# Loading w_in in rows of 128 in a fused attention, gated MLP and soft mixture kernel

## The chip, the cores and the metric

The kernel runs on one core of a Trainium2 chip. The metric is the device time of one execution in microseconds, the median of the runs.

## What is computed

Three layers follow each other in float32: a causal attention with a decay per head, in blocks with a running state; an MLP with a gate; and a soft mixture of eight small experts.

```python
# q, k, v: [2, 8, 768, 64]; lam: [8]
intra = einsum('bhic,bhjc->bhij', qb, kb) * Dmask     # lam ** (i - j), i >= j
inter = einsum('bhid,bhde->bhie', qb * lam_pow, kv_state)
out[:, :, sl] = einsum('bhij,bhjd->bhid', intra, vb) + inter
kv_state = lam_block * kv_state + einsum('bhsd,bhse->bhde', kb * rev_pow, vb)
# x: [1536, 512], a column is 64 * head + d
h = x @ w_in                                          # [512, 2048]
x = (h * clip(h + 3, 0, 6) / 6) @ w_out               # [2048, 512]
# soft mixture: 8 experts of 4 slots, w1 [8, 512, 1024], w2 [8, 1024, 512]
logits = x @ phi; d = softmax(logits, 0); c = softmax(logits, 1)
out = c @ experts(d.T @ x)
```

`w_in` and `w_out` arrive as float64, 8 MB each; the kernel makes float32 of them on the chip. The rest is float32.

## The kernel before, in words

**Tiles.** The 1536 tokens are 12 tiles t of 128 (six of each batch). Attention works with a block C = 128. `w_in` is cut into NF = 4 groups n of 512 columns and KT = 4 slices kt of 128 rows of the contraction; the 16 pieces are loaded as raw pairs of int32 words (`load_w_in`, L433), 4 KB a row, and turned to float32 by ScalarE and VectorE in `convert` (L577: L583, L590, L597, L604), then split in two float32r parts `whi` and `wlo` (L622). One unit h(t, n) is 12 matmuls of 128x512 (`h_unit`, L1008), in two halves of 6.

**Attention of a tile** (`attention`, L774). q and k arrive as [128 tokens, 8 heads, 64] (`load_qkv`, L409). TensorE transposes pairs of heads (L793), so a pair lies in the two halves of the partitions; ScalarE copies them out (`tr`, L810). `ps` are the scores of both halves (L862), `pm` the scores times the decay mask (VectorE, L870), `pv` the products that update the state (L883, weights k times `rev`, moving v), `px` the output, from the state (L900) and from `pm` (L907). x then has the heads in rows: slice kt holds two heads, one in each half of the partitions. `lamq` and `rev` hold powers of lam for the heads; `selp` places them (L350).

Before, the transposed pair is heads 2a and 2a+1, while slice kt of x holds heads kt and kt+4. So the rows of w_in that belong to a slice are two runs of 64, and `load_w_in` issues two transfers of 64 rows for each piece (L435 to L441). The 64x64 products with the state take their operands from the half h2 of the pair.

**Order.** Every step is an `Op` with an engine, a number in the order in which it was made, its dependencies and buffers. `ORDER` (L73) is a list of these 943 numbers written out by hand; `Plan.run` (L187) walks it, gives out ring buffers (46 of 4 KB a partition) with a table of assumed durations, and issues. So each engine's program has the order of the list. DMA issues marked `free` go to SP, or to ACT when their number is in `BY_ACT` (L123). All other loads go to SP's queue. A transfer's issue waits on SP for its buffer.

**The start of SP's list before:** w_in (0,1) as two transfers, k of tile 0, w_in (0,0) and (1,0), `pw_d` (a store of the powers of lam), q0, k1, w_in (0,3) and (0,2), q1, the two halves of the mask `dec` (read back from `pw_d`), v0, q2, k2, v1, k3, q3, w_in (1,1), v2, k4, q4, w_in (1,3), (1,2), (3,0), v3, w_in (2,0), (3,2), q7, q5, k5, and so on.

**The end.** After the last h units the experts' weights (64 loads of 512 KB on 128 rows, L1322 and L1332) are multiplied, and the result is stored.

Of the kernel before, what the change touches and what calls it, by code (L numbers as in the profile page):

```python
# [121 lines left out]
)  # L122
BY_ACT = (421, 709, 885, 918, 939,)  # L123
# [134 lines left out]
def attn_moe_softmoe_kernel(  # L258
# [60 lines left out]
    T = {}  # L319
# [15 lines left out]
    while m < C:  # L335
# [18 lines left out]
        base=0, pattern=[[-2, NPAIR], [-1, 2], [0, 64]], channel_multiplier=1,  # L354
# [57 lines left out]
    def load_qkv(x, t):  # L412
        b, c = divmod(t, NC)
        name, i = {"q": ("qk", 0), "k": ("qk", 1), "v": ("vd", 0)}[x]

        def fn():
            if (name, t) not in T:
                T[name, t] = rtile([128, 2, H, D], f"{name}{t}")
            QUEUE[plan.eng].dma_start(  # L419
                out=T[name, t][:, i],  # L420
                in_={"q": q, "k": k, "v": v}[x][b, :, C * c : C * c + C].rearrange(
                    "h p d -> p h d"
                ),
            )

        take = [] if (name, t) in bufs else [ring_buf((name, t))]
        ops["ld" + x, t] = load(
            fn, KB512 / 2, take=take, rel=[] if take else [bufs[name, t]], eff=0.58, rows=64,
            **queue(f"{x}{t}"),
            reserve=load_reserve,  # L430
        )

    def load_w_in(n, kt):  # L433
        def fn():
            T["wraw", n, kt] = rtile([128, 512, 2], f"wraw{n}_{kt}", I32)  # L435
            for i in range(2):
                r = D * (KT * i + kt)
                QUEUE[plan.eng].dma_start(  # L438
                    out=T["wraw", n, kt][D * i : D * i + D].rearrange("p f w -> p (f w)"),
                    in_=w_in.bitcast(I32)[r : r + D, 1024 * n : 1024 * n + 1024],  # L440
                )  # L441

        ops["ldw", n, kt] = load(
            fn, KB512, take=[ring_buf(("wraw", n, kt))], reserve=load_reserve, eff=1.1, n=2,
            **queue(f"w{n}_{kt}"),
        )
# [87 lines left out]
    def make_rev():  # L534
        DVE.tensor_copy(rev, T.pop("rev_p"))  # L535
# [238 lines left out]
    def attention(t, prio):  # L774
# [91 lines left out]
        def f_pm(g):  # L866
            def fn():
                if ("pm", t) not in T:
                    T["pm", t] = rtile([128, H, C], f"pm{t}")
                DVE.tensor_tensor(  # L870
                    out=T["pm", t].rearrange("p (a g) c -> p g a c", g=2)[:, g],
                    in0=T["ps", t][g],
                    in1=T["dec"].rearrange("p (a g) c -> p g a c", g=2)[:, g], op=ALU.mult,
# [4 lines left out]
        def f_pv():  # L878
            vd = T["vd", t]
            pv = T["pv", t] = ptile(v_tag, [128, NPAIR, D], f"pv{t}")  # L880
            for h in range(H):
                p, h2 = divmod(h, 2)
                PE.matmul(  # L883
                    pv[64 * h2 : 64 * h2 + 64, p], lhsT=vd[:, 1, h], rhs=vd[:, 0, h],
                    start=True, stop=True,
                )

        def bank(kt):
            return T["px", t, kt % 2][:, kt // 2] if c > 0 else T["px", t, 0][:, kt]

        def f_px():
# [4 lines left out]
            for kt in range(KT if c > 0 else 0):  # L896
                for i in range(2):
                    p, h2 = divmod(KT * i + kt, 2)
                    r = slice(64 * h2, 64 * h2 + 64)
# [824 lines left out]
```

## Time and profile before

| | us |
|---|---|
| median of 3 runs | 309.9 (309.62 to 311.62) |
| the profiled execution | 310.75 |
| its span, first to last instruction | 308.9 |
| TensorE (PE) busy | 277.1 |
| VectorE (DVE) busy | 198.8 |
| ScalarE (ACT) busy | 122.8 |
| mean granted clock of TensorE | 0.955 |

The profile is of one execution. PE are matmuls, PEld weight loads, SPq the instructions of SP's queue (DMA issues). L-numbers are lines of the kernel. Start times count from the span's start. In the table by stretch, the columns are the stretch, its length, then for PE, PEld, DVE, ACT and POOL the busy time (and count), the granted clock of TensorE as a share of full speed, the mean busy share of the 16 DMA engines, and GB/s. "[7.82 <-X]" at the end of a timeline row is the idle time of the engine before it, and what ended it. A float32 matmul shows as two instructions.

### The profile page before, as it was taken

How to read it: one execution, taken by the hardware profiler on the slowest of the kernel's cores; microseconds unless marked ns; L12 is line 12 of the kernel's file. 1: busy time of each engine (PE TensorE's matmuls, PEld its weight loads, DVE VectorE, ACT ScalarE, POOL GpSimd, SP SyncE). 2: the span in 40 equal slices, each digit the busy share in tenths (PEclk: the TensorE clock that was granted, in tenths of full speed). 3: DMA queues.
4: the chain of work that ended last, by engine and by line, in shares of the span. 5: the costliest groups of instructions: out<-in, count | busy, mean ns of one | idle time of the engine just before them, and what ended most of it. 6: DMA issues, size and time to landing. Idle time of an engine off the chain costs nothing.

```text
span 308.9 us, 7313 instructions
## 1 busy us (share of the span) xinstructions
PE 277.1 (90%) x2956; PEld 210.1 (68%) x2956; DVE 198.8 (64%) x330; ACT 122.8 (40%) x235; POOL 36.3 (12%) x51
## 2 busy tenths in 40 slices
PE   6269994999879899999999999999999998979990
PEld 5268883878657788788667768668776756556670
DVE  3368894799946999998987796675633216213151
ACT  3454555988347657312131232224124241111240
POOL 4034210423202602000110010100000000000000
PEclk9578998899959999999999999999999999999997
DMA  7999999999996765667896768999799999999987
GB/s 145 221 234 210 208 213 179 241 293 317 219 215 181 249 181 153 168 155 191 194 262 162 205 152 197 227 306 358 243 334 417 395 408 342 389 407 407 313 262 235
DMA packets 79217, 78.67 MB, mean 255 GB/s; under 512 B 41800, under 2 KB 67920, under 8 KB 79184
## 3 DMA queue, kind: packets, MB, share of 16 engines
q1 hardware_dynamic: 76704, 76.37, 88.1%
q10 hardware_dynamic: 2480, 1.84, 2.1%
q8 instruction: 23, 0.38, 0.5%
q14 instruction: 10, 0.08, 0.1%
HBM read 60.36 MB, written 3.15 MB: 206 GB/s over the span
## 4 chain that ended last, share of the span: by engine, by line
PE 63%; DMA 17%; SPq 10%; DVE 4%; issue 1%; ACT 1%; POOLq 0%; DVEq 0%; ACTq 0%
PE h L1019 35%; SPq L419 5%; SPq L438 4%; DMA wo_raw<-in_moe_w_out_dram 4%; PE po L1574 4%; DMA e<-in_moe_w_dram 4%; PE lg L1125 3%; DMA qk<-in_q_dram 3%; PE p L1540 3%; PE pd L1240 3%; PE ps L862 3%; DMA wraw<-in_moe_w_in_dram 2%; PE pt L793 2%; PE px L907 2%; DMA qk<-in_k_dram 2%; DMA gq<-gb 2%
## 5 line engine op out<-in xcount | busy, mean ns | idle before, releaser
L1019 PE MATMUL h<-whi,x 128*128 128x512 f32 x384 | 124.1, 405 | 0.6 <-DVE g L1039 0.6
L1019 PEld LDWEIGHTS h<-whi,x 128*128 128x128 f32 x384 | 70.8, 191 | 17.6 <-issue 2.0
L1019 PE MATMUL h<-wlo,x 128*128 128x512 f32 x192 | 75.9, 395 | 0.0
L1033 ACT ACTIVATE g<-h,half_b 128x512 f32<-128x512 f32 x48 | 33.0, 688 | 53.1 <-PE h L1019 37.4
L1039 DVE SCALAR_TENSOR_TENSOR g<-g,h 128x512 f32<-128x512 f32 x48 | 32.6, 678 | 29.3 <-ACT g L1033 25.9
L1102 DVE STREAM_TRANSPOSE gb<-g 128x1024 f32<-128x1024 f32 x20 | 40.9, 2053 | 5.3 <-POOL vd L849 2.5
L1019 PEld LDWEIGHTS h<-wlo,x 128*128 128x128 f32 x192 | 36.6, 191 | 8.3
L793 PE MATMUL pt<-ident,qk 128*128 128x128 f32 x96 | 15.8, 308 | 13.8 <-DMA qk<-in_q_dram 13.8
L793 PEld LDWEIGHTS pt<-ident,qk 128*128 128x128 f32 x96 | 12.1, 155 | 17.4 <-DMA qk<-in_q_dram 8.0
L931 POOL TENSOR_TENSOR states<-states,lamq 64x256 f32<-64x256 f32 x16 | 10.7, 669 | 88.9 <-DVE states L944 80.7
L810 ACT COPY tr<-pt 128x512 f32<-128x512 f32 x24 | 13.6, 582 | 17.9 <-PE pt L793 9.5
L870 DVE TENSOR_TENSOR pm<-ps,dec 128x512 f32<-128x512 f32 x24 | 15.7, 681 | 7.2 <-ACT tmp_o L590 4.0
L862 PE MATMUL ps<-tr 64*128 64x128 f32 x192 | 15.9, 306 | 3.2 <-ACT tr L810 3.0
L862 PEld LDWEIGHTS ps<-tr 64*128 64x128 f32 x192 | 13.3, 207 | 7.1 <-ACT tr L810 3.5
L583 ACT ACTIVATE tmp_i<-wraw 128x512 f32<-128x512 f32 x16 | 10.5, 670 | 18.9 <-DMA wraw<-in_moe_w_in_dram 14.5
L1559 DVE STREAM_TRANSPOSE ht<-hsi 128x256 f32<-128x256 f32 x8 | 5.1, 651 | 19.6 <-ACT hsi L1551 19.6
L1540 PE MATMUL p<-e,hsi 128*32 128x256 f32 x256 | 15.2, 381 | 2.1 <-DMA e<-in_moe_w_dram 1.6
L710 DVE STREAM_TRANSPOSE wb<-wo_f 128x1024 f32<-128x1024 f32 x8 | 16.1, 2022 | 0.1
L849 POOL TENSOR_TENSOR vd<-qk,rev 128x512 f32<-128x512 f32 x10 | 11.0, 1112 | 42.8 <-DVE rev L535 12.8
L1574 PE MATMUL po<-e,ht 128*32 128x128 f32 (+1 forms) x384 | 15.4, 309 | 0.3 <-DMA e<-in_moe_w_dram 0.3
L633 POOL TENSOR_TENSOR wlo<-tmp_i,whi 128x512 fp32r<-128x512 f32 x8 | 11.2, 1419 | 25.4 <-ACT whi L630 25.3
L1574 PEld LDWEIGHTS po<-e,ht 128*32 128x32 f32 x384 | 11.1, 110 | 4.4 <-DMA e<-in_moe_w_dram 0.5
(115 smaller groups left out, 341.9 us busy)
## 6 DMA issues: line engine op xcount, KB each, us to landing
e<-in_moe_w_dram SPq DMA_DIRECT2D x64, 512.0 KB, 7.1
gq<-gb SPq DMA_DIRECT2D x76, 128.0 KB, 2.8
wraw<-in_moe_w_in_dram SPq DMA_DIRECT2D x32, 256.0 KB, 6.6
wo_raw<-in_moe_w_out_dram SPq DMA_DIRECT2D x16, 512.0 KB, 6.0
wq<-wb SPq DMA_DIRECT2D x28, 128.0 KB, 2.7
qk<-in_k_dram SPq DMA_DIRECT2D x12, 256.0 KB, 5.8
qk<-in_q_dram SPq DMA_DIRECT2D x12, 256.0 KB, 7.0
vd<-in_v_dram SPq DMA_DIRECT2D x12, 256.0 KB, 7.3
```

Of the source, the lines that this page charges most:

```text
L419: QUEUE[plan.eng].dma_start(out=T[name, t][:, i], in_={"q": q, "k": k, "v": v}[x][b, :, C * c : C * c + C].rearrange("h p d -> p h d"),)
L710: DVE.transpose(out=x.rearrange("p q d c f -> p c d q f"), in_=y.rearrange("p c (d t q) -> p c d q t", d=KT, q=4),)
L793: PE.transpose(p[:, a], x[:, i, 2 * a : 2 * a + 2].rearrange("p a d -> p (a d)"), ident,)
L810: ACT.copy(T["tr", t][:, i], T["pt", t, i])
L862: PE.matmul(ps[g][:, p], lhsT=z[r, p], rhs=y[r, p], start=True, stop=True)
L870: DVE.tensor_tensor(out=T["pm", t].rearrange("p (a g) c -> p g a c", g=2)[:, g], in0=T["ps", t][g], in1=T["dec"].rearrange("p (a g) c -> p ...
L1019: PE.matmul(ph, lhsT=xt[:, a, kt], rhs=T[w, n, part][:, kt % 2], start=i == 0, stop=i == 3 * KT - 1,)
L1033: ACT.activation(T["g", tp, n][:, i], T["h", t, n], AF.Relu, bias=half_b, scale=1.0 / 6.0)
L1039: DVE.scalar_tensor_tensor(out=to, in0=to, scalar=1.0, in1=T.pop(("h", t, n)), op0=ALU.min, op1=ALU.mult,)
L1102: DVE.transpose(out=x.rearrange("p q c i t -> p i c q t"), in_=T["g", tp, n].rearrange("p i (c t q) -> p i c q t", c=4, q=4),)
L1540: PE.matmul(p1[32 * j : 32 * j + 32], lhsT=T["sit"][:, b4], rhs=T["e1", e, b4][:, 256 * j : 256 * j + 256], start=b4 == 0, stop=b4 == 3,)
L1574: PE.matmul(T["po", hf][32 * qd : 32 * qd + 32], lhsT=T["ht", e // 4][:, e % 4, b8], rhs=T["e2", e, b8 // 2][:, b8 % 2, lo:hi] if e < WHOL ...
```

## The change

- `load_w_in`: one transfer of 128 rows for a piece, instead of two of 64.
- `load_qkv`: q and k by two transfers each, of four heads. Heads h and h+4 stand side by side, so the pair that is transposed is (a, a+4). v stays one transfer.
- `make_rev`, `selp`, `f_pm`: the same sizes with the new order of heads.
- `f_pv`: heads 0 to 3 go to the lower half of the partitions of `pv`, heads 4 to 7 to the upper; the loop still counts h up.
- `f_px`: kt in the order 0, 2, 1, 3 for the products with the state; the two PSUM banks now hold slices (0, 1) and (2, 3) instead of (0, 2) and (1, 3).
- `ORDER` and `BY_ACT` are new. The start of SP's list: k0, w_in (0,1), q0, `pw_d`, k1, q1, w_in (0,0), (0,2), the first half of `dec`, v0, q2, k2, w_in (0,3), v1, k3, q3, w_in (1,2), v2, (1,0), k4, q4, (1,1), v3, (1,3), (3,0), two pieces of w_out, (3,2), q5, v4, k5. The second half of `dec` (number 8) is issued by ACT, after the two conversions of w_in (0,1) and ahead of the copy of q0's transposes. On TensorE the operations ahead of the first h are the same set. The transposes of tile 5 stood behind seven halves of h units, and stand behind ten.

```diff
 ORDER = (
-    10, 0, 252, 253, 2, 9, 246, 248, 247, 73, 18, 6, 4, 76, 270, 254, 77, 255, 3, 271,
+    73, 0, 76, 74, 77, 2, 75, 10, 252, 4, 6, 3, 5, 253, 254, 255, 78, 9, 11, 7,
...
 )
-BY_ACT = (421, 709, 885, 918, 939,)
+BY_ACT = (8, 409, 626, 703, 885, 918,)
...
-        base=0, pattern=[[-2, NPAIR], [-1, 2], [0, 64]], channel_multiplier=1,
+        base=0, pattern=[[-1, NPAIR], [-4, 2], [0, 64]], channel_multiplier=1,
...
-            QUEUE[plan.eng].dma_start(
-                out=T[name, t][:, i],
-                in_={"q": q, "k": k, "v": v}[x][b, :, C * c : C * c + C].rearrange(
-                    "h p d -> p h d"
-                ),
-            )
+            src = {"q": q, "k": k, "v": v}[x][b, :, C * c : C * c + C].rearrange("h p d -> p h d")
+            if x == "v":
+                QUEUE[plan.eng].dma_start(out=T[name, t][:, i], in_=src)
+                return
+            to = T[name, t][:, i].rearrange("p (a g) d -> p g a d", g=2)
+            for g in range(2):
+                QUEUE[plan.eng].dma_start(
+                    out=to[:, g], in_=src[:, NPAIR * g : NPAIR * g + NPAIR]
+                )
...
-            for i in range(2):
-                r = D * (KT * i + kt)
-                QUEUE[plan.eng].dma_start(
-                    out=T["wraw", n, kt][D * i : D * i + D].rearrange("p f w -> p (f w)"),
-                    in_=w_in.bitcast(I32)[r : r + D, 1024 * n : 1024 * n + 1024],
-                )
+            QUEUE[plan.eng].dma_start(
+                out=T["wraw", n, kt].rearrange("p f w -> p (f w)"),
+                in_=w_in.bitcast(I32)[
+                    128 * kt : 128 * kt + 128, 1024 * n : 1024 * n + 1024
+                ],
+            )
...
-                    out=T["pm", t].rearrange("p (a g) c -> p g a c", g=2)[:, g],
+                    out=T["pm", t].rearrange("p (g a) c -> p g a c", g=2)[:, g],
...
-                p, h2 = divmod(h, 2)
+                g, p = divmod(h, NPAIR)
                 PE.matmul(
-                    pv[64 * h2 : 64 * h2 + 64, p], lhsT=vd[:, 1, h], rhs=vd[:, 0, h],
+                    pv[64 * g : 64 * g + 64, p], lhsT=vd[:, 1, 2 * p + g], rhs=vd[:, 0, h],
...
-            return T["px", t, kt % 2][:, kt // 2] if c > 0 else T["px", t, 0][:, kt]
+            return T["px", t, kt // 2][:, kt % 2] if c > 0 else T["px", t, 0][:, kt]
...
-            for kt in range(KT if c > 0 else 0):
+            for kt in (0, 2, 1, 3) if c > 0 else ():
                 for i in range(2):
-                    p, h2 = divmod(KT * i + kt, 2)
-                    r = slice(64 * h2, 64 * h2 + 64)
+                    g, p = divmod(2 * kt + i, NPAIR)
+                    r = slice(64 * g, 64 * g + 64)
...
-                    h = KT * i + kt
+                    h = 2 * kt + i
```

## Rows read from the trace of the kernel before

**Rows 1.** Table by stretch, in us from the start, and its sum.

```profile
0.00:28.30 28.30, 17.07 (x129) 15.84 (x130) 14.32 (x32) 12.38 (x21) 8.04 (x22) 0.76 1.07 203
28.30:49.10 20.80, 20.51 (x237) 16.75 (x235) 17.66 (x33) 12.70 (x24) 4.18 (x6) 1.00 1.05 209
49.10:61.00 11.90, 8.23 (x46) 6.63 (x45) 6.95 (x14) 7.90 (x16) 3.29 (x4) 0.86 0.95 204
61.00:83.70 22.70, 22.70 (x192) 18.27 (x191) 22.48 (x37) 17.51 (x31) 6.96 (x6) 1.00 1.09 280
83.70:103.00 19.30, 14.66 (x160) 11.45 (x158) 12.50 (x22) 11.33 (x19) 3.22 (x3) 0.82 0.80 193
...
sum 308.90, PE 277.13 PEld 210.14 DVE 198.75 ACT 122.83 POOL 36.31; mean PE 30.79 PEld 23.35 DVE 22.08 ACT 13.65 POOL 4.03
```

**Rows 2.** Timeline of TensorE's matmuls, 0 to 60 us.

```profile
13.63 1.97 PE L793 MATMUL pt<-ident,qk 128*128 128x128 f32 x8 [7.82 <-DMA qk<-in_q_dram]
...
28.33 0.71 PE L1019 MATMUL h<-whi,x 128*128 128x512 f32 x2
...
33.08 0.73 PE L1019 MATMUL h<-whi,x 128*128 128x512 f32 x2
```

**Rows 3.** Chain that ended last, in order of time: start, us, what.

```profile
42.97 9.69 DMA qk<-in_q_dram
52.66 0.14 issue
52.80 2.09 PE pt L793 x8
...
63.47 0.87 PE pt L793 x8
...
74.04 11.81 DMA wo_raw<-in_moe_w_out_dram
...
104.26 0.46 PE pv L883 x16
```

**Rows 4.** Timeline of ScalarE, 80 to 90 us.

```profile
85.96 0.66 ACT L583 ACTIVATE tmp_o<-wo_raw 128x512 f32<-128x512 f32 x1 [5.70 <-DMA wo_raw<-in_moe_w_out_dram]
86.53 0.57 ACT L810 COPY tr<-pt 128x512 f32<-128x512 f32 x1
```

**Rows 5.** DMA view of the stretches 22:28, 36:42 and 240:250, in this order.

```profile
DMA packets 5160, 1.32 MB, mean 220 GB/s; under 512 B 5159, under 2 KB 5159, under 8 KB 5159
...
DMA packets 466, 1.40 MB, mean 234 GB/s; under 512 B 130, under 2 KB 130, under 8 KB 465
...
DMA packets 1098, 4.01 MB, mean 401 GB/s; under 512 B 120, under 2 KB 120, under 8 KB 1098
```

**Rows 6.** A timeline row of SP's queue, and a DMA issue group (median to landing).

```profile
88.80 5.30 SPq L723 DMA_DIRECT2D wq<-wb  x8
...
wq<-wb SPq DMA_DIRECT2D x28, 128.0 KB, 2.7
```

**Rows 7.** Timeline of SP's queue (DMA issues), 0 to 16 us.

```profile
1.22 1.20 SPq L438 DMA_DIRECT2D wraw<-in_moe_w_in_dram  x2
2.46 0.60 SPq L419 DMA_DIRECT2D qk<-in_k_dram  x1
3.10 2.81 SPq L438 DMA_DIRECT2D wraw<-in_moe_w_in_dram  x4
6.04 0.41 SPq L469 DMA_DIRECT2D pw_d<-rp  x1
6.49 0.38 SPq L419 DMA_DIRECT2D qk<-in_q_dram  x1
...
7.98 5.94 SPq L438 DMA_DIRECT2D wraw<-in_moe_w_in_dram  x4
...
14.60 1.13 SPq L476 DMA_DIRECT2D dec<-pw_d  x2
15.77 3.40 SPq L419 DMA_DIRECT2D vd<-in_v_dram  x1
```

**Rows 8.** Waits of SP's queue: us in total, times, longest.

```profile
SPq L1322 <- PE h L1019: 13.0, 8, 4.7
```

More of the change, by code (lines that the diff above doesn't have):

```diff
@@ L428, in load_qkv @@
             fn, KB512 / 2, take=take, rel=[] if take else [bufs[name, t]], eff=0.58, rows=64,
+            n=1 if x == "v" else 2,
             **queue(f"{x}{t}"),
@@ L435, in fn @@
             T["wraw", n, kt] = rtile([128, 512, 2], f"wraw{n}_{kt}", I32)
-            for i in range(2):
-                r = D * (KT * i + kt)
-                QUEUE[plan.eng].dma_start(
-                    out=T["wraw", n, kt][D * i : D * i + D].rearrange("p f w -> p (f w)"),
-                    in_=w_in.bitcast(I32)[r : r + D, 1024 * n : 1024 * n + 1024],
-                )
+            QUEUE[plan.eng].dma_start(
[4 more added lines that the diff above has]
+            )
         ops["ldw", n, kt] = load(
-            fn, KB512, take=[ring_buf(("wraw", n, kt))], reserve=load_reserve, eff=1.1, n=2,
+            fn, KB512, take=[ring_buf(("wraw", n, kt))], reserve=load_reserve, eff=1.1,
             **queue(f"w{n}_{kt}"),
@@ L534, in make_rev @@
     def make_rev():
-        DVE.tensor_copy(rev, T.pop("rev_p"))
+        DVE.tensor_copy(
+            rev.rearrange("p (a g) -> p g a", g=2),
+            T.pop("rev_p").rearrange("p (g a) -> p g a", g=2),
+        )
     def make_lamq():
@@ L870, in fn @@
                 DVE.tensor_tensor(
-                    out=T["pm", t].rearrange("p (a g) c -> p g a c", g=2)[:, g],
+                    out=T["pm", t].rearrange("p (g a) c -> p g a c", g=2)[:, g],
                     in0=T["ps", t][g],
-                    in1=T["dec"].rearrange("p (a g) c -> p g a c", g=2)[:, g], op=ALU.mult,
+                    in1=T["dec"].rearrange("p (g a) c -> p g a c", g=2)[:, g], op=ALU.mult,
                 )
@@ L895, in f_px @@
                 T["px", t, 1] = ptile("g", [128, 2, C], f"px{t}_1")
-            for kt in range(KT if c > 0 else 0):
+            for kt in (0, 2, 1, 3) if c > 0 else ():
                 for i in range(2):
-                    p, h2 = divmod(KT * i + kt, 2)
-                    r = slice(64 * h2, 64 * h2 + 64)
+                    g, p = divmod(2 * kt + i, NPAIR)
+                    r = slice(64 * g, 64 * g + 64)
                     PE.matmul(
                         bank(kt)[64 * i : 64 * i + 64], lhsT=old[r, p, r],
-                        rhs=T["trd", t][r, p], start=kt < 2, stop=False,
+                        rhs=T["trd", t][r, p], start=kt % 2 == 0, stop=False,
                     )
@@ L905, in f_px @@
                 for i in range(2):
-                    h = KT * i + kt
+                    h = 2 * kt + i
                     PE.matmul(
                         bank(kt)[64 * i : 64 * i + 64], lhsT=vd[:, 0, h], rhs=P[:, h],
-                        start=c == 0, stop=c == 0 or kt >= KT - 2,
+                        start=c == 0, stop=c == 0 or kt % 2 == 1,
                     )
@@ L915, in parts @@
                 return [(x[:, 0], x[:, 1], T["px", t, 0])]
-            y = x.rearrange("p w (a b) c -> p w a b c", b=2)
-            return [(y[:, 0, :, b], y[:, 1, :, b], T["px", t, b]) for b in range(2)]
+            return [
+                (x[:, 0, 2 * b : 2 * b + 2], x[:, 1, 2 * b : 2 * b + 2], T["px", t, b])
+                for b in range(2)
+            ]
         def f_xh():
```

94 rows, old and new, of the table ORDER are left out of this document.

## The prediction

> **What bounds the kernel now.** Read the table by stretch first [rows 1]. Of the span of 308.9 us TensorE has 277.1 us busy; of the 31.8 us that it misses, 19.8 lie ahead of 103 us: 11.2 before 28.3, where the first h matmul stands (28.30 - 17.07), 3.7 in the stretch from 49.1, 4.6 in the one from 83.7. The same stretches have the lower clock: 0.76, 0.86 and 0.82 of full speed as means of its two levels, where the others have 1.00. In them the DMA engines are busy for 0.80 to 1.07 of the time at only 193 to 204 GB/s. So the front is a kernel waiting for transfers.
>
> Next, what TensorE waits for. It opens its first transposes at 13.63 us after 7.82 us of waiting for q, and the first h at 28.33 [rows 2]. In the chain [rows 3] a q issued at 42.97 lands 9.69 us later, and TensorE stands until 52.80; a wo_raw issued at 74.04 takes 11.81 us, and ScalarE sits 5.70 us for it at 85.96 [rows 4] with the copy of the next tr queued behind.
>
> Then what a transfer costs while the queue is full [rows 5]: the stretch 22:28 is q, k and v alone (220 GB/s, so 262,144 B take 1.19 us); 36:42 is nearly all w_in on 64 rows (234 GB/s, 1.12 us a half, 2.24 us a tile); 240:250 is expert weights on 128 rows (401 GB/s, 1.31 us for 512 KB). The expert rows are 4 KB as well, and w1 lies in memory with the same 16 KB step as w_in, so of what the kernel sets only the number of rows written differs.
>
> **The change, part by part.**
>
> *w_in on 128 rows.* Sixteen pairs of 256 KB become sixteen loads of 512 KB. I take 1.31 us a tile from the expert loads: 2.24 - 1.31 = 0.93 us, 14.9 us over the 16 tiles. Bounds: nothing saved (the 64-row rate stays) and 14.9. I take the upper end because the shape, row length and step are those of the expert row.
>
> The Trainium skill speaks here with two voices. "SBUF — State Buffer", section "Door 1: The DMA port swizzle", says bandwidth goes by how many of 16 ports the partitions reach, and 64 rows in a half reach only half of them; the trace agrees (234 against 401 GB/s). "DMA: Bandwidth & Descriptors", section "Rules for kernel authors", says that two transfers to the two halves use the same 16 engines and so serialise; by that alone a merged load would save just an issue, and the sum would lose its 14.9 us. The rows decide for the first.
>
> *q and k by two transfers each.* 24 loads become 48 of 128 KB; 24 issues more, 16 fewer for w_in, so SP issues 8 more. A 128 KB transfer costs SP 0.66 us (5.30 us for eight, and it lands after 2.7 us, so no queue builds) [rows 6]; 1.19 / 2 = 0.60 us is the DMA's own part. I take no change of the DMA time; the bounds are 0 and +0.59 us a half. Issue is hidden as long as the queue is full (before, the v load at 15.77 holds SP 3.40 us) [rows 7].
>
> *The new order at the start.* Before q of tile 0 stood six halves of w_in, k and q (2 + 4 halves, [rows 7]): 6 x 1.12 + 2 x 1.19 = 9.1 us. Now one tile, k and q: 1.31 + 2.38 = 3.7. The transposes open 5.4 us earlier, at 8.2. The first h needs px of tile 0 and so v: ahead of v stood ten halves (11.2 us), now three tiles (3.9 us), with the same k0, q0, k1, q1 and dec. So 7.3 us earlier: h opens at 21.0 instead of 28.3. Its work ahead is the same list of operations in both orders. **Term A: -7.3.** Two waits are moved into this stretch. The second dec load is now ACT's, queued there ahead of the copy of q0: ACT waits for the store pw_d to land. That store took between 2.7 us (the 128 KB row) and 8.6 (issued at 6.04, read at 14.60), and goes out at about 5; near 2.7 ACT is free by about 8.2, with the issue, before the transposes are done. I take that and no cost; at the far end the copy comes at 13.5 and about 3 us of A go. And w0_3 now comes after q2 and k2: from 8.2 on five loads of 1.19, three tiles of 1.31 and dec at 1.2 each, so at 20.5; the second half of the first h unit, 4.75 us after the first in the trace of before, would want it at 25.8, and 5 us are left for its conversions. I charge nothing.
>
> *The stop at 49.1.* By the k load of tile 5 the old list has eleven tiles of w_in, the new one ten and two of w_out: 24.6 against 15.7 us, 8.9 earlier. Term A has TensorE there 7.3 earlier, but three more h halves (about 1.4 each) now stand ahead of these transposes. The stop goes: 3.7 idle and the slow clock after it, 0.14 x 8.23 = 1.2. **Term B: -4.9.**
>
> *The stop at 83.7.* In the old list the wo_raw of 74.04 follows two tiles of w_in that were still in the queue; these alone bring its landing 1.9 us nearer, and the 13 tiles ahead of them have left 12.1 us earlier, against a wait of 5.70. Idle 4.6 plus 0.18 x 14.66 = 2.6 of slow clock: 7.2 at most. What is late next is DVE: from 28.3 to 103 it works 59.6 of 74.7 us; without TensorE's idle time (8.6) and slow clock (3.8) that stretch is 62.3 us, 96% for DVE. It has run so (22.48 of 22.70 from 61.0), but in program order and with other work to wait for. I take half. **Term C: -3.6**, bounds 0 and -7.2.
>
> *pv loses its alternation.* Before, the eight heads of pv went to the two column halves in turn; now four run in one half, then four in the other. Sixteen instructions take 0.46 us, 29 ns each [rows 3]. Where weights are loaded into the columns that were just used, the nearest row is the transposes: 0.87 us for eight, 109 ns with 128 columns, so 54 ns with 64: 0.87 us a pv. Bounds 0 and +0.41. I take the upper end, since that row has the same reuse; ten pv, of which two stand in the waiting stretch: **term D: +3.3.** The px products keep their alternation.
>
> The skill's "TensorE: Matmul & The Clock Gate", section "LDWEIGHTS (loading the stationary operand)", gives columns / 1.2 ns: an estimate of 53 ns for 64. The trace's 29 ns a pair can only be had if loads of the two halves overlap; by that rule the new order costs 0.38 us a pv, near term D.
>
> Copies and masks only change strides; sizes and counts stay: nothing. After 103 us TensorE misses 12.0 of 206 us, and the expert loads wait for buffers that h frees (13.0 us of SP's waits) [rows 8], so they come forward with it, and the rest keeps its length.
>
> Sum: 308.9 - 7.3 - 4.9 - 3.6 + 3.3 = 296.4 us of span. The profiled execution was 310.75, 1.85 above its span; the median of the runs is 309.9, 1.0 above that span. On the median: **297.4**.
>
> **Rivals.**
> - *Everything goes, pv is free* (C whole, D nothing): 308.9 - 7.3 - 4.9 - 7.2 = 289.5, 290.5 on the median. For it: DVE's 99% from 61.0 to 83.7. Against: reuse of columns.
> - *Only the start* (the lead of the transfers stops at full buffers, or at DVE): 308.9 - 7.3 + 3.3 = 304.9, 305.9 on the median. For it: DVE's 96%. Against: at 49.1 nothing but q is missing.
> - *The change doesn't do what it says*: 128 rows keep 234 GB/s. Then only the order is left, four halves fewer ahead of v: -4.5 + 3.3, 308.7. Against: the expert loads' 401.
> - *Slower: a half of q or k takes as long as the whole*, 1.19 us. Through tile 8, 18 pairs then cost 21.4 us more, w_in gives 14.9, pv takes 3.3: +9.8, 319.7. It decides from 0.91 us a half: 18 x (2 x 0.91 - 1.19) + 3.3 = 14.6. Against: rows 6, which move 128 KB every 0.66 us.
>
> **How the numbers follow.** Forecast 0.50, everything 0.17, only the start 0.17, no wider rows 0.08, slower 0.08. The range, 290 to 306, takes the first three, with bounds of C and D; it leaves out 0.16 and strays. About 1% (3 us) is what a measurement here can tell from no change. Faster by over 1%: 0.50 + 0.17 + 0.14 (most of only the start) = 0.81; within 1%: 0.08 + 0.03 = 0.11; slower: 0.08.
>
> **What would show it.** w_in at some 400 GB/s in its stretches; first transposes near 8 us, first h near 21; no wait of TensorE for q of tile 5; no 5.70 us wait of ScalarE for wo_raw; sixteen pv instructions in 0.87 us instead of 0.46. Wrong if h opens after 25, if DVE's idle time from 28 to 103 stays at 15 us, or if q and k land below 200 GB/s.

## The result, and the profile after

| | before | after |
|---|---|---|
| median (us), four runs of each, taken together | 310.76 (309.62 to 313.10) | 293.58 (292.84 to 295.84) |
| the profiled execution, its span | 310.75, 308.9 | 294.15, 292.1 |
| TensorE busy, idle in the span | 277.1, 31.8 | 275.7, 16.4 |
| VectorE busy | 198.8 | 196.2 |

The ratio is 0.945, 95% interval [0.937, 0.953]: faster, and by 3.8 us more than the forecast of 297.4, inside the range. The span lost 16.8 us; 15.4 of them are TensorE's idle time, 1.4 its busy time. In e2, e6 and e8 below, one execution each lay over 1.5% above the fastest (in e2 the profiled one, 311.07 us); without it their medians are 308.75, 294.54 and 294.66 us.

The table by stretch, cut at the first h and at 103 us; it answers to [rows 1]:

```profile
0.00:22.70 22.70, 18.37 (x131) 17.00 (x131) 12.61 (x30) 9.84 (x17) 7.15 (x20) 0.92 0.89 229
22.70:103.00 80.30, 78.94 (x728) 64.65 (x726) 74.38 (x126) 62.50 (x110) 24.29 (x25) 1.00 0.90 267
103.00:292.00 189.00, 178.37 (x2102) 130.18 (x2101) 109.22 (x176) 49.99 (x110) 4.55 (x6) 0.99 0.87 275
sum 292.00, PE 275.68 PEld 211.84 DVE 196.22 ACT 122.33 POOL 35.99; mean PE 91.89 PEld 70.61 DVE 65.41 ACT 40.78 POOL 12.00
```

From the first h to 103 us TensorE now misses 1.4 us (80.30 - 78.94) and its clock is 1.00 all the way; before, it missed 8.6 there, at a clock of 0.86 and 0.82 in the two of its four stretches that had the stops. Ahead of the first h it misses 4.3 instead of 11.2. After 103 it misses 10.6 instead of 11.9.

A cut through the densest part, 50 to 90 us, shows DVE beside it: 38.17 of 40.00 us busy, and TensorE still has 38.64.

```profile
50.00:90.00 40.00, 38.64 (x394) 31.32 (x393) 38.17 (x62) 31.97 (x58) 13.40 (x13) 1.00 0.86 259
```

The longest waits of TensorE (us in total, times, longest), first the longest of before, then those of after. The 13.8 us for q are down to 0.4, and the longest stop is one for the mask product `pm`, at the start:

```profile
PE pt L793 <- DMA qk<-in_q_dram: 13.8, 3, 7.8
```

```profile
PE ps L869 <- DVE pm L877: 2.8, 1, 2.8
PE h L1028 <- DVE g L1048: 1.3, 1, 1.3
...
PE pt L800 <- DMA qk<-in_q_dram: 0.4, 1, 0.4
```

The timeline of TensorE after, which answers to [rows 2]: the transposes open at 7.45, the first h at 22.68. The score product of tile 1 comes after 2.84 us of standing still and takes 2.49 us, where the one of tile 0 took 1.16; the px behind it takes 1.87.

```profile
7.45 1.94 PE L800 MATMUL pt<-ident,qk 128*128 128x128 f32 x8 [0.38 <-DMA qk<-in_q_dram]
...
10.93 1.16 PE L869 MATMUL ps<-tr 64*128 64x128 f32 x16
...
16.86 2.49 PE L869 MATMUL ps<-tr 64*128 64x128 f32 x16 [2.84 <-DVE pm L877]
19.28 1.87 PE L914 MATMUL px<-pm,vd 128*64 128x128 f32 x16
20.98 0.92 PE L890 MATMUL pv<-vd 128*64 128x64 f32 x16
...
22.68 0.71 PE L1028 MATMUL h<-whi,x 128*128 128x512 f32 x2
```

The chain that ended last, after [rows 3]: q and its 9.69 us are gone from it, a `dec` load of 7.76 us stands near its head, wo_raw still comes once but with 5.42 us instead of 11.81, and sixteen pv take 0.74 us instead of 0.46.

```profile
8.18 7.76 DMA dec<-pw_d
...
16.63 0.69 DVE pm L877
17.37 1.99 PE ps L869 x14
19.35 1.80 PE px L914 x16
...
27.03 0.74 PE pv L890 x16
...
70.41 5.42 DMA wo_raw<-in_moe_w_out_dram
```

ScalarE's longest stop for wo_raw, 5.70 us in [rows 4], is 1.54:

```profile
75.94 0.69 ACT L590 ACTIVATE tmp_o<-wo_raw 128x512 f32<-128x512 f32 x1 [1.54 <-DMA wo_raw<-in_moe_w_out_dram]
```

The DMA views of 34:36 and 36:38 after, in this order, answer to the 234 GB/s of [rows 5]. Nearly all of it is rows of 4 KB on 128 partitions; in the first stretch mostly tiles of w_in (two land at 35.66 and, in the second stretch, 36.76), in the second mostly w_out.

```profile
DMA packets 204, 0.75 MB, mean 373 GB/s; under 512 B 22, under 2 KB 22, under 8 KB 204
...
DMA packets 225, 0.82 MB, mean 410 GB/s; under 512 B 25, under 2 KB 25, under 8 KB 225
```

That is 1.28 to 1.41 us for 512 KB, about the forecast's 1.31. These two stretches were taken because hardly anything else moves in them; where the 256 B pieces of q, k and v mix in, the rate is lower (336 GB/s over 28 to 40).

The DMA issues of the page after, and the first of SP's issues in its timeline; they answer to [rows 6] and [rows 7]:

```profile
wraw<-in_moe_w_in_dram SPq DMA_DIRECT2D x16, 512.0 KB, 5.8
...
qk<-in_k_dram SPq DMA_DIRECT2D x24, 128.0 KB, 4.3
qk<-in_q_dram SPq DMA_DIRECT2D x24, 128.0 KB, 4.0
```

```profile
1.21 0.95 SPq L425 DMA_DIRECT2D qk<-in_k_dram  x2
2.21 0.50 SPq L440 DMA_DIRECT2D wraw<-in_moe_w_in_dram  x1
2.75 0.98 SPq L425 DMA_DIRECT2D qk<-in_q_dram  x2
```

A pair of 128 KB halves costs SP 0.95 to 0.98 us. The k and q halves land after 4.3 and 4.0 us, where the whole ones took 5.8 and 7.0 in the profile before (medians, in another order of loads).

### The profile page after: what moved, and what is told of

Read it like the earlier page. It is cut to its first block, busy times and chain, and to the rows that moved or that the text cites. A ratio compares the mean times of both kernels' runs of the same rounds, so it can differ in the third digit from the quotient of the medians.

```text
span 292.1 us, 7338 instructions
## 1 busy us (share of the span) xinstructions
PE 275.7 (94%) x2956; PEld 211.8 (73%) x2956; DVE 196.2 (67%) x330; ACT 122.3 (42%) x235; POOL 36.0 (12%) x51
## 4 chain that ended last, share of the span: by engine, by line
PE 69%; DMA 15%; DVE 7%; SPq 3%; issue 2%; ACT 2%; DVEq 0%; ACTq 0%
PE h L1028 39%; DMA e<-in_moe_w_dram 10%; PE lg L1134 4%; PE px L914 4%; PE pd L1249 4%; PE ps L869 4%; DMA dec<-pw_d 3%; PE pt L800 2%; PE pv L890 2%; DMA wo_raw<-in_moe_w_out_dram 2%; PE px L907 2%; SPq L1355 2%; PE w2p L742 1%; PE pg L1093 1%; PE pt L1652 1%
## 5 line engine op out<-in xcount | busy, mean ns | idle before, releaser
L1028 PE MATMUL h<-whi,x 128*128 128x512 f32 x384 | 121.8, 398 | 1.3 <-DVE g L1048 1.3
L1028 PEld LDWEIGHTS h<-whi,x 128*128 128x128 f32 x384 | 69.8, 188 | 17.0 <-DVE g L1048 1.9
L1028 PE MATMUL h<-wlo,x 128*128 128x512 f32 x192 | 75.0, 391 | 0.0
L817 ACT COPY tr<-pt 128x512 f32<-128x512 f32 x24 | 13.7, 580 | 11.3 <-PE pt L800 7.2
L856 POOL TENSOR_TENSOR vd<-qk,rev 128x512 f32<-128x512 f32 x10 | 11.6, 1161 | 54.8 <-DMA gq<-gb 27.6
L869 PE MATMUL ps<-tr 64*128 64x128 f32 x192 | 15.2, 295 | 3.0 <-DVE pm L877 2.8
L869 PEld LDWEIGHTS ps<-tr 64*128 64x128 f32 x192 | 12.7, 196 | 7.1 <-ACT tr L817 4.2
L1583 PE MATMUL po<-e,ht 128*32 128x128 f32 (+1 forms) x384 | 16.3, 309 | 1.6 <-DVE ht L1568 0.8
L940 POOL TENSOR_TENSOR states<-states,lamq 64x256 f32<-64x256 f32 x16 | 10.6, 662 | 56.5 <-DVE states L953 53.0
L717 DVE STREAM_TRANSPOSE wb<-wo_f 128x1024 f32<-128x1024 f32 x8 | 16.4, 2046 | 0.1
L800 PE MATMUL pt<-ident,qk 128*128 128x128 f32 x96 | 15.1, 294 | 0.4 <-DMA qk<-in_q_dram 0.4
L1568 DVE STREAM_TRANSPOSE ht<-hsi 128x256 f32<-128x256 f32 x8 | 5.0, 641 | 14.7 <-ACT hsi L1560 9.8
L611 DVE SCALAR_TENSOR_TENSOR tmp_i<-tmp_i 128x512 int32<-128x512 int32 x16 | 13.2, 828 | 1.4 <-ACT tmp_i L597 1.1
L640 POOL TENSOR_TENSOR wlo<-tmp_i,whi 128x512 fp32r<-128x512 f32 x8 | 10.5, 1318 | 27.9 <-ACT whi L637 22.1
```

Source lines behind the costliest of these rows:

```text
L611: DVE.scalar_tensor_tensor(out=lw if dst is None else dst(), in0=hp, scalar=3, in1=lw, op0=ALU.logical_shift_left, op1=ALU.bitwise_or,)
L717: DVE.transpose(out=x.rearrange("p q d c f -> p c d q f"), in_=y.rearrange("p c (d t q) -> p c d q t", d=KT, q=4),)
L800: PE.transpose(p[:, a], x[:, i, 2 * a : 2 * a + 2].rearrange("p a d -> p (a d)"), ident,)
L817: ACT.copy(T["tr", t][:, i], T["pt", t, i])
L869: PE.matmul(ps[g][:, p], lhsT=z[r, p], rhs=y[r, p], start=True, stop=True)
L1028: PE.matmul(ph, lhsT=xt[:, a, kt], rhs=T[w, n, part][:, kt % 2], start=i == 0, stop=i == 3 * KT - 1,)
```

## The experiments

The runs answer four questions: which part of the change brings the time (rows, number of transfers, order); what pv's new order costs; what holds the first h; and whether splitting q and k costs anything. The edits are against the changed kernel; its own control runs are c_after and c2_after.

### e2_rows_of_64: the old rows in the new kernel

```diff
-            QUEUE[plan.eng].dma_start(
-                out=T["wraw", n, kt].rearrange("p f w -> p (f w)"),
...
+            for i in range(2):
+                r = 128 * kt + D * i
+                QUEUE[plan.eng].dma_start(
+                    out=T["wraw", n, kt][D * i : D * i + D].rearrange("p f w -> p (f w)"),
+                    in_=w_in.bitcast(I32)[r : r + D, 1024 * n : 1024 * n + 1024],
+                )
```

> The changed kernel, with each piece of w_in loaded by two transfers of 64 rows again (rows 0 to 63 and 64 to 127 of the slice, 4 KB each); new order and everything else kept. Theory (a transfer that writes only 64 rows runs at 234 instead of 400 GB/s, and this is most of the gain): 0.93 us a piece is back, the first h comes about 2.8 us later (three pieces are ahead of v), TensorE waits for transfers again between 40 and 90 us, and the span is 8 to 14 us longer, 300 to 306. Rival (the gain is the new order): at most 1.5 us longer, 292 to 294.

Measured: 309.08 us, ratio to before 0.992 [0.988, 0.996]. Nearly all of the gain is gone with the rows; the loss, 15.5 us, is more than the 8 to 14 expected. The first h stands at 23.89, 1.2 to 3.0 us later than in the three profiles of the changed kernel. The table by stretch and TensorE's waits show where the rest is:

```profile
22.70:50.00 27.30, 22.96 (x244) 19.18 (x243) 19.57 (x36) 16.16 (x31) 5.87 (x8) 0.94 1.08 217
50.00:90.00 40.00, 33.03 (x247) 26.14 (x245) 30.13 (x50) 25.86 (x45) 7.89 (x7) 0.99 1.03 237
```

```profile
PE ps L869 <- ACT tr L817: 7.5, 4, 3.1
PE pt L800 <- issue: 3.6, 1, 3.6
PE pt L800 <- DMA qk<-in_k_dram: 1.9, 1, 1.9
```

The DMA engines are busy all the time (1.08, 1.03) at 217 and 237 GB/s, where the changed kernel has 259 in 50:90 with engines 0.86 busy. TensorE misses 11.3 us from 22.7 to 90. Its 7.5 us for `tr` on ScalarE are waits at one remove: ScalarE stands 26.4 us in all for w_in, with the copies of `tr` queued behind its conversions:

```profile
L590 ACT ACTIVATE tmp_i<-wraw 128x512 f32<-128x512 f32 x16 | 10.8, 674 | 26.4 <-DMA wraw<-in_moe_w_in_dram 26.4
```

In the DMA view of 40:46, nearly all w_in, the rate is the old one. The engines do not stand idle in it: a single packet of 4 KB takes 282 ns there in the median, and 159 ns in the changed kernel from 34 to 38.

```profile
DMA packets 438, 1.40 MB, mean 233 GB/s; under 512 B 99, under 2 KB 99, under 8 KB 437
```

### e4_half_columns: still two transfers, but of 128 rows

Each piece in two transfers of 128 rows and half the columns (2 KB of a row), so the bytes of a transfer and their number are those of e2.

```diff
+            for i in range(2):
+                x = 1024 * n + 512 * i
+                QUEUE[plan.eng].dma_start(
+                    out=T["wraw", n, kt][:, 256 * i : 256 * i + 256].rearrange("p f w -> p (f w)"),
+                    in_=w_in.bitcast(I32)[128 * kt : 128 * kt + 128, x : x + 512],
+                )
```

> The changed kernel, with each piece of w_in loaded by two transfers of 128 rows and 2 KB a row (half the columns each): as many transfers and bytes a transfer as with 64 rows, but all 128 rows are reached. Theory (the rows reached set the rate): w_in stays at 350 to 400 GB/s and the span within 2 us of 292.1. Rival (one transfer of 512 KB is better than two of 256 KB, whatever the rows): w_in falls towards 234 GB/s and the span goes to 300 or more, as with rows of 64.

Measured: 293.61 us, ratio 0.946 [0.940, 0.952]: the changed kernel's time. So the time isn't lost to the number of transfers, nor to their size: with the same number and size as in e2, the rows reached (and the length of a row) differ, and 15.5 us with them. The shorter rows do cost rate: from 33 to 38 us, mostly w_in and w_out, e4 moves 287 GB/s where the changed kernel moves 384, less than the 350 to 400 expected; the time doesn't show it.

The Trainium skill's page "SBUF — State Buffer", section "Door 1: The DMA port swizzle", says that DMA bandwidth depends on how many of the 16 ports the partitions of a transfer reach; the two runs agree with that, as do the 233 GB/s of e2 beside the 373 above. The ports themselves no run shows. A transfer of 64 rows also reads half as many rows of memory, and no run separates that from the partitions written.

### e3_old_order: the new loads in the old order

```diff
-BY_ACT = (8, 409, 626, 703, 885, 918,)
+BY_ACT = (421, 709, 885, 918, 939,)
```

and the whole of `ORDER` is that of the kernel before.

> The changed functions (w_in in rows of 128, q and k by two transfers, the heads paired h and h+4) with ORDER and BY_ACT of the kernel before. Theory (rows): w_in at about 400 GB/s; five pieces stand ahead of v, so the first h comes 4.6 us earlier than before, at about 24; the stops at 49 and 84 us shrink or go; with pv 2.8 us longer the span is 296 to 301. Rival (order): the span is that of before or longer, 307 to 312, since the old list has the same pieces ahead of what TensorE waits for.

Measured: 296.09 us, ratio 0.953 [0.948, 0.959]. The first h is where it was expected, and the span, 294.1, is 2 us under the 296 to 301 expected. TensorE's timeline opens later than with the new order, after a wait for q:

```profile
11.06 1.97 PE L800 MATMUL pt<-ident,qk 128*128 128x128 f32 x8 [4.22 <-DMA qk<-in_q_dram]
...
24.13 0.71 PE L1028 MATMUL h<-whi,x 128*128 128x512 f32 x2
```

With e2 that makes a square: old order and 64 rows 310.8, new order and 64 rows 309.1, old order and 128 rows 296.1, both new 293.6. The rows are worth 14.7 to 15.5 us in either order, the order 1.7 to 2.5 with either rows. The two parts very nearly add up.

### e5_qk_one: q and k by one transfer each

```diff
-            to = T[name, t][:, i].rearrange("p (a g) d -> p g a d", g=2)
-            for g in range(2):
-                QUEUE[plan.eng].dma_start(
-                    out=to[:, g], in_=src[:, NPAIR * g : NPAIR * g + NPAIR]
-                )
+            QUEUE[plan.eng].dma_start(out=T[name, t][:, i], in_=src)
```

> The q and k pieces by one transfer each, so the heads stand in the order of memory (0 to 7) and not as h beside h+4: the attention reads other heads' columns than it should, the work and its sizes are unchanged. 24 or more issues of 128 KB fall away. Theory (the halves run side by side on SP's queue and their issues, 0.43 to 0.51 us each, are hidden behind transfers already under way): within 1 us of the changed kernel, 292.6 to 294.6. Rival (SP's issues set when the late transfers begin): 12 q and k issues in the first 22 us, at 0.45 us each some 5 us of SP, come out of the start, and the first h opens 2 us or more earlier: 291.5 or less. The other rival (the transfers of 1 KB rows gain in size by being one): the queue's rate in the stretch 40 to 46 rises and the time stays.

Measured: 293.49 us, ratio 0.943 [0.940, 0.947], beside 293.26 of the control. The first h opens at 21.57, the control's at 21.25. Splitting q and k costs nothing that shows, and SP's issues didn't set the start. The rate in 40 to 46 didn't rise either: 228 GB/s, against 277 and 250 in two profiles of the changed kernel.

### e1_pv_in_turns and f_turns: the alternation given back

```diff
-            for h in range(H):
+            for h in (0, 4, 1, 5, 2, 6, 3, 7):
```

> The changed kernel, with only the loop of pv taking the heads in the order 0, 4, 1, 5, 2, 6, 3, 7, so that the two column halves alternate again. In the profile after, pv takes 0.74 us (0.75 and 0.92 where the clock is low or mixed) against 0.46 before. Theory (weights that go into the columns just used cannot be loaded beside the matmul): pv is back at 0.46 us, ten times 0.28 us, and since TensorE is hardly idle after 22 us the span falls by some 2.5 us, to about 289.5 (median about 291). Rival (pv is longer because of its operands, or the time is hidden): pv stays at 0.74 us, or falls and the span stays within 0.5 us of 292.1.

Measured: 292.03 us, ratio 0.941 [0.935, 0.947]. The groups by line: pv of the changed kernel, then of this one. Ten groups of sixteen are 2.8 us shorter, and with the same operands: the order of the heads alone does it.

```profile
L890 PE MATMUL pv<-vd 128*64 128x64 f32 x160 | 9.2, 225 | 0.0
```

```profile
L890 PE MATMUL pv<-vd 128*64 128x64 f32 x160 | 6.4, 222 | 0.0
```

The single records of the trace say how. In the changed kernel the sixteen instructions start one by one, 58 ns apart, except in the middle, where the half changes: there three pairs start 4 to 6 ns apart, which leaves thirteen steps (0.74 us). With the heads in turn they start in pairs all along, a pair every 58 ns: eight steps (0.46 us).

The interval overlaps the changed kernel's (0.937 to 0.953), and the first h of this profile stands at 20.52 against 22.68, so a part of the difference could be the start. It was measured once more, beside a control.

> The changed kernel a third time, beside the next two on the same chip: 293.3 us, between 292.3 and 294.5.

> The kernel with the state products in turns again, now beside the changed kernel on one chip. Its TensorE work is 3.6 us less than the changed kernel's in the profiles so far (272.1 against 275.7 us), but TensorE also stood idle 1.5 to 2.3 us longer (17.9 against 15.6 and 16.4 us). Theory (the work saved lies on the path in the part where TensorE never stops, and only there): 1 to 2 us less than the changed kernel, 291.3 to 292.3. Rival (DVE or the loads are next in line, the saving comes back as waits): within 0.7 us of it.

Measured: the control 294.22 us (292.03 to 295.73), 0.9465 [0.942, 0.951]; the turns 292.52 (290.60 to 293.21), 0.9392 [0.935, 0.943]. So 1.7 us between the medians, though the ranges still overlap, from 292.0 to 293.2: pv's time most likely lies on the path, and some 60% of the 2.8 shows. Part of the rest came back as idle time behind the first h, where TensorE is 24.96 of 27.30 us busy; the control has 26.03 there.

```profile
22.70:50.00 27.30, 24.96 (x263) 20.14 (x259) 23.70 (x44) 19.76 (x36) 6.78 (x9) 1.00 1.02 301
```

### c_after: the start of the same kernel once more

> The changed kernel once more, beside the next three. Expected: 293.6 us in the median, as before, between 292.5 and 295.5; its first h between 20.5 and 22.7 us. If the first h scatters between runs of this same kernel, its scatter goes with the granted clock of the first 22.7 us (0.92 in the one execution, 1.00 in the one of the kernel with the turns).

Measured: 293.26 us (291.33 to 294.51), 0.941 [0.937, 0.945]. Its timeline has the second score product at 1.16 us, with no stop ahead of it, and the first h at 21.25; in the third profile of the same kernel, c2_after, the h stands at 20.88. The rows of the one, then of the other:

```profile
12.48 2.08 PE L869 MATMUL ps<-tr 64*128 64x128 f32 x16
...
17.54 1.16 PE L869 MATMUL ps<-tr 64*128 64x128 f32 x16
...
21.25 0.71 PE L1028 MATMUL h<-whi,x 128*128 128x512 f32 x2
```

```profile
10.67 2.08 PE L869 MATMUL ps<-tr 64*128 64x128 f32 x16
...
16.67 1.66 PE L869 MATMUL ps<-tr 64*128 64x128 f32 x16 [0.72 <-DVE pm L877]
...
20.88 0.71 PE L1028 MATMUL h<-whi,x 128*128 128x512 f32 x2
```

So the 22.68 of the first profile is the late end of a scatter. There the granted clock from 16.0 to 22.7 has a mean of 0.75, that is the lower of its two levels in part, after 2.84 us in which TensorE did nothing; ps and px took (2.49 - 1.16) + (1.87 - 1.09) = 2.1 us more than at full clock. In c_after and c2_after it is 1.00 in that stretch. These two ran slowly earlier instead: their first score product took 2.08 us where the first profile has 1.16 (in c2_after the granted clock is 0.50 from 10 to 14). That seems to have cost less: TensorE was busy longer ahead of the second score product, and stood still there for 0 and 0.72 us instead of 2.84.

### e6_dec_first, e7_both and e8_tiles_first: what holds the first h

The first profile named `dec` as what the mask product waits for. e6 moves its two loads ahead of two tiles of w_in:

```diff
-    ... 78, 9, 11, 7, 8, 80, ...
+    ... 78, 7, 8, 9, 11, 80, ...
```

> Only the place of the two dec loads is moved: ahead of the w_in rows of k-tile 0 and 2 (steps 0,0 and 0,2) in the written order. Theory (the start fell short of the forecast by 1.7 us because the mask product waits for dec, which takes 7.8 us from its issue, and TensorE stands idle there until its clock drops): dec lands 2 to 3 us earlier, the first mask product starts at 13.5 to 14.5 instead of 16.0, the granted clock of the first 22.7 us is 1.00, the first h opens between 19.5 and 21, and the whole is 291.5 to 292.5. Rival (dec is only the last of several loads that land together; the w_in rows moved back now open the first h): the first mask product is earlier, the first h stays between 22 and 24, and the time stays within 0.7 us of the changed kernel's.

Measured: 294.70 us, 0.9465 [0.943, 0.950], the control 293.26: nothing gained. The theory fell: the first h stands at 22.72, and the granted clock from 16.0 to 22.7 is 0.75 again. The chain of this kernel shows what took the place of `dec`: a tile of w_in, with ScalarE's conversions of it, and the copy of tile 1's transposes queued behind these.

```profile
8.40 7.20 DMA wraw<-in_moe_w_in_dram
...
15.62 0.67 ACT tmp_i L590
...
16.29 0.67 ACT tmp_i L597
16.96 0.44 ACT tr L817
...
17.44 1.52 PE ps L869 x16
```

And the first mask product, whose `dec` had landed, stood on VectorE behind the same tiles' conversions until 15.97, against 16.02 in the changed kernel.

e7 has both this and the turns.

> Both edits: the state products in turns (heads 0,4,1,5,...) and dec ahead of the w_in rows. Theory: the turns bring the ten groups of state products from 0.74 back to 0.46 us, ten times 0.28 = 2.8 us less TensorE work, of which 1.5 to 2.8 show; with dec early another 1.5 to 2: 289 to 290.5 us. Rival (the turns' gain in the one run was the start's clock alone, so the two edits are one gain): 291.5 to 292.3, the same as with dec alone.

Measured: 293.47 us, 0.942 [0.938, 0.945]: 1.2 below e6, about what the turns give, and not below the turns alone. Both expected ranges lie under it.

e8 goes on from e7 and puts tile 1's copies, on ScalarE, and tile 0's mask products, on VectorE, ahead of the conversions:

```diff
-    ... 85, 246, 247, 248, 91, 93, 249, 92, 258, 260, 14, 15, 259, 82, 94, 95, 12, 250, 83, 13, 84, 96, ...
+    ... 85, 91, 92, 93, 82, 94, 95, 246, 247, 83, 84, 248, 249, 258, 260, 14, 15, 259, 12, 250, 13, 96, ...
```

> With the turns, and three moves in the written order: dec ahead of the w_in rows of k-tile 0 and 2; the copies of tile 1's transposes ahead of the conversions of those rows on ScalarE; the mask products of tile 0 ahead of them on VectorE. Theory (dec alone gave nothing because the copies of tile 1, queued on ScalarE behind conversions that wait for w_in, opened next; with both moved, the chain of attention runs on without the w_in rows): second score product at 15 to 16 us instead of 16.6 to 17.5, first h at 19 to 20, and 0.5 to 1.5 us less than with the turns alone. Rival (the conversions, now behind the mask products, then hold the first h back): the first h stays at 20.5 to 22 and the time within 0.7 us of the turns alone, or above it.

Measured: 294.69 us, 0.9445 [0.940, 0.949], 2.2 above the turns. The mask product came forward by three us and the second score product to 15.92, as expected, and then the conversions were late, and behind them on VectorE the second mask product and x. VectorE's timeline, then TensorE's second h instruction:

```profile
13.08 1.29 DVE L877 TENSOR_TENSOR pm<-ps,dec 128x512 f32<-128x512 f32 x2 [0.69 <-PE ps L869]
...
17.64 0.69 DVE L640 TENSOR_TENSOR wlo<-tmp_i,whi 128x512 fp32r<-128x512 f32 x1 [0.59 <-ACT whi L637]
...
19.45 1.28 DVE L877 TENSOR_TENSOR pm<-ps,dec 128x512 f32<-128x512 f32 x2
20.65 0.68 DVE L935 TENSOR_TENSOR x<-px,x 128x512 fp32r<-128x512 f32 x1
```

```profile
21.39 0.50 PE L1028 MATMUL h<-whi,x 128*128 128x512 f32 x1 [0.71 <-DVE x L935]
```

So no single load holds the first h. The last loads ahead of it (two tiles of w_in, `dec` and v) land between 11 and 17 us in all of these profiles of the new order, and 0 to 16 moves 220 to 233 GB/s in them; in the orders tried, whichever was put first made another the last, and the work behind them on ScalarE and VectorE filled the rest. What would bring the start further forward was not found.

## Why the prediction was right, and where its terms were off

*Rows of 128 (2.24 to 1.31 us a tile): right.* 373 to 410 GB/s against the expert loads' 401, and e2 and e4 give the 15 us to going from 64 rows to 128, not to fewer or larger transfers. Of the two rules of the Trainium skill weighed there, a run now decides as well as a row: if transfers to the two halves lost only by serialising, which is the reason given in "DMA: Bandwidth & Descriptors", section "Rules for kernel authors", e2 would lie within a few issues of the changed kernel, and it is 15.5 us slower.

*Term A, the start: -7.3 forecast, -5.65 in the profile, and -7.1 and -7.5 in the other two (28.33 - 21.25, 28.33 - 20.88).* The transposes came at 7.45 (8.2 forecast). ACT's `dec` went out at 7.56, right behind its conversions, and its copies were 0.99 us behind TensorE: the moved wait cost nothing, as taken. What I hadn't priced is that the start has several ends within a microsecond or two of each other, so that in one execution TensorE stood for 2.84 us and ran on at the lower clock.

*Terms B and C, the stops at 49.1 and 83.7: -4.9 and -3.6 forecast.* Both are gone. From the first h to 103 us the idle time fell from 8.6 to 1.4 and the clock from a loss of 3.8 (1.2 and 2.6, as the prediction worked it out) to none: -11.0 against -8.5 for the two. The step that failed is "I take half": VectorE's 96% was to be late next. VectorE did come next. It ran at 95% (38.17 of 40.00), and the chain that ended last goes over it and its waits from 38.7 to 51.6 us. But all that it cost TensorE was 1.3 us, once, the wait for `g` above, not 3.6. The 99% of the stretch from 61.0 in the kernel before had been a hint at that.

*Term D, pv: +3.3 forecast, on eight of ten.* The mechanism was right, e1 and f_turns undo it; the size was not: +0.28 us a pv, not 0.41. The price of a step in one half was nearly right, 58 ns where 54 were halved from the transposes. What failed is that it was counted for all sixteen instructions: where the half changes, three pairs start together, so thirteen steps are left. The Trainium skill's rule in "TensorE: Matmul & The Clock Gate", section "LDWEIGHTS (loading the stationary operand)", gives 53 by estimate; the measured 58 decides. Of ten times 0.28, 1.7 show in the time.

*After 103 us: nothing forecast, and TensorE's idle time fell by 1.3.* Where from stays open. SP's wait for h in front of the expert loads fell from the 13.0 of [rows 8] to 5.4:

```profile
SPq L1331 <- PE h L1028: 5.4, 3, 2.4
```

But other releasers took its place: all of SP's waits at this line come to 28.5 us after and 24.3 before.

The sum over the span from the first h on: idle 7.2 + 1.3, less busy time 2.75 (18.37 of 275.68 lie ahead of the h after, 17.07 of 277.13 before), in all 11.3, and 5.65 at the start: 16.9, the 16.8 measured. The clock's part is inside the 2.75: with nine pv longer by 0.28 (+2.5), some 5.2 us of slow clock should have gone, 3.8 of them foreseen; the other 1.4 stay unplaced. Against the forecast of 296.4 for the span that is +1.65 at the start, -2.5 at the two stops, -0.8 for pv, -1.3 after 103 us and the -1.4 unplaced: 292.05, and 292.1 was measured. The start of this one execution made up for some of the rest; that is luck.

*SP's issues, 0.66 us for 128 KB:* 0.48 here, and hidden (e5).

*The rivals.* "Everything goes, pv free" came nearest in time, 290.5, and half of it is right: C is whole, pv is not free; the turns make it free and reach 292.5. "Only the start" falls with the idle time from 22.7 to 103. "128 rows keep 234 GB/s" was put at 308.7; e2 is that kernel and gives 309.1. "Slower" falls with e5: two halves cost no more time than the whole.

The version with the turns is the fastest of those tried, 292.03 and 292.52 us against 293.58, 293.26 and 294.22 of the changed kernel. The step from one to the other, 1.7 us side by side, is under the 3 us that the prediction took for what a measurement can tell from no change; it rests on three comparisons of one sign (e1, f_turns, and e7 against e6).

## What to carry to other kernels

Where a front waits for loads and the DMA engines are always busy at a low rate, compare the rate with that of the best transfer elsewhere in the same trace, and look at how many partitions a transfer writes before touching its order: here rows gave 15 us and a wholly new order 2. A new layout that lets the transfers be wide may break an alternation elsewhere; that is one line in the loop over heads to give back. When a wait names a load, move it forward once; if another load then takes its place at the same time, as in the orders tried here, the stage is probably bound by their sum, and more reordering promises little.

## What the runs showed that was not expected

- Two transfers of 128 rows by 2 KB give the time of one of 128 by 4 KB (293.61 against 293.58 us), though at a lower rate (287 against 384 GB/s from 33 to 38), while two of 64 rows by 4 KB don't (309.08): the number and the size of transfers didn't matter to the time in this range.
- Sixteen instructions of 64 weight columns take 0.46 us when the heads alternate between the column halves and 0.74 when they don't; a step takes 58 ns in both, but starts two instructions in the first case and mostly one in the second.
- TensorE lost 2.1 us of the start in one of three profiles of one kernel, by the lower clock after a 2.84 us stop; in the other two it ran slowly earlier, ahead of that stop, and the first h came sooner. The first h of these three profiles scatters from 20.88 to 22.68.
